# Attention and a mixture of experts: the third list's search moved, its rows turned by VectorE behind a DRAM scratch, one round's weight remainders subtracted on GpSimd

## Chip, cores and metric

One core of a Trainium2 chip runs the whole program. The metric is device time in microseconds (us) of one execution; the time given for a kernel is the median of its runs.

## What is computed

Attention over 8 batches, 8 heads, 576 positions and 64 columns with two masks (a window of 32, and a window of 128 at every fourth position), then a mixture of experts on its 4608 x 512 result. The routing is greedy over all (token, expert) pairs in falling order of the gate's logits, with 576 places for each expert:

```python
x = attn_out.transpose(0, 2, 1, 3).reshape(4608, 512)
logits = x @ w_gate                              # 4608 x 8
for idx in np.argsort(-logits.flatten()):
    tok, e = idx // 8, idx % 8
    if assigned[tok] >= 0 or counts[e] >= 576:
        continue
    assigned[tok] = e
    counts[e] += 1
for e in range(8):
    mask = assigned == e
    out[mask] = np.maximum(x[mask] @ w1[e], 0.0) @ w2[e]     # w1 512 x 1024, w2 1024 x 512
```

## The kernel before

The attention comes first (`attention`, to about 178 us of the span) and writes x to DRAM (`xd`) row by row. One expert's list is found by `alone` without anything beside it. After that the kernel runs eight rounds; round r computes one expert's 576 tokens, and the lists of later rounds are searched on VectorE beside the products of the rounds before.

**A round's products.** Everything is multiplied in pairs of a high part (rounded to the short float format of TensorE's fast path) and a low part (what the rounding left), so each product is three: high by high, high by low, low by high. The first product (`first`, L1460) makes 1024 hidden rows in eight pieces f, each for 256 (j = 0) and 320 (j = 1) tokens: per piece and j 12 instructions of 256 or 320 columns. The second (L1506, L1509, L1511) runs over five blocks m of 128, 128, 128, 128 and 64 tokens: 112 instructions of 512 columns. All of this is one chain on TensorE in the order of the rounds.

**What a round needs.** (1) Its list: `search(r)` makes eight steps. In each, TensorE counts (`counts`, L841, nine small matmuls) what VectorE flagged (`step`, L889 to L899, and the flags G, L853, L855 or L1176). Then `members`, `ranks` (TensorE), `accept`, `digits`; then `within` (six instructions that write `ob`, VectorE), `by_chunk` (`rx`, GpSimd, L1181) and `by_row` (ScalarE) feed `place` (TensorE, L1195), and `indices` (VectorE, L1204 to L1207) leaves the list as row numbers `idx`. (2) Its rows x: `gather` fetches them with one indirect DMA a block, issued by GpSimd. In rounds 0 to 2 (r < QUARTERS) TensorE turns a block with four transposes into PSUM (`ptx`, L1396), ScalarE writes the high part `xh` from there and VectorE the low part `xl` (L1245). From round 3 on `spread` is used: the gathered block goes to a DRAM scratch (`ROWS`, L1420) and comes back in four pieces (L1424), so arranged that one VectorE transpose of 32 x 32 squares (L1430) ends with the tokens along the free axis; the weights are then read from a copy of W1 with its rows permuted alike (`in_moe_w1q`). (3) Its weights: `weights` loads 128 x 512 blocks into `raw`, ScalarE writes the high part, and the low part is either subtracted by VectorE (L1245) or, for the pairs in ADDED, written as minus the high part by ScalarE (L1271) and then completed by a GpSimd DMA that adds `raw` onto it (L1273).

**What sets the order.** `Schedule` plans all engines ahead from a table of costs and due times: each operation has a cost, dependencies, and a boost that makes it due earlier, and the finished plan is the fixed order of each engine. T_P is the assumed cost of one count, B_C the boost of the search of list r, B_L that of the list's making, AHEAD the number of rounds that a search may run ahead. In `search`, `hold` is what a search must wait for; for r = 2 it is the first product of round 1.

```python
hold = gemm1_end.get(r - AHEAD) if r != 2 else gemm0[1]
g = prev + [hold]
```

**Queues.** SyncE (SP) issues the plain transfers in its planned order: the weights, the scratch stores and loads, and a register load of the expert's number (`fetch`) that waits for the end of a search. GpSimd issues the gathers, the adding DMAs and the scatters of the results (`put`, L1532), each behind a memset of `spacer`.

Of the kernel before, what the change touches and what calls it, by code (L numbers as in the profile page):

```python
# [32 lines left out]
NM = 5  # L33
# [4 lines left out]
HI16, LO16 = -4128832, 4128831  # L38
HIGH = 65536.0
TOL_DVE, TOL_ACT, TOL_POOL, TOL_PE, T_W = 100, -50, 200, 500, 730  # L40
T_P, T_S, AHEAD = 310, 2200, 5
B_L, B_G, B_T, B_X, B_H, B_HL, B_Y, B_S, B_W = 23000, 27000, 15000, 0, 20000, 17000, 28000, -15000, 1500
RAW1, D_R, NQ, AHEAD_W = 8, 262, (2, 2), (3, 4)
QUARTERS, POOLED, T_B, T_H, B_R = 3, range(0), 5000, 2500, 20000
ADDED, T_A, T_G, T_L = (("2", 0), ("1", 1), ("2", 1)), 4500, 4500, 3500
T_D = {"1": 5000, "2": 4000}
NS, B_E, DIRECT, T_I = (2, 2), 3000, 7, 5000
B_C = (0, 2500, *(20000 + -16000 * (r >= QUARTERS) for r in range(2, 8)))
P_U, B_A, B_K, B_V, B_P, TOL_A, TOL_B, TOL_C, TOL_D = 4680, 15400, -5200, 14500, -105500, 650, 650, 300, 800
Q_ENG = (("POOL", "POOL", "POOL", "ACT"), ("DVE", "DVE", "ACT", "ACT"))  # L50
MSZ = (128, 128, 128, 128, 64)
# [119 lines left out]
class Schedule:  # L171
# [9 lines left out]
    def op(self, eng, cost, fn, deps=(), boost=0, lat=0, dma=0, buf=None, mode=64, tail=None):  # L181
        x = Op(len(self.ops), eng, cost, fn, deps, boost, lat, dma, buf)
        x.mode = mode
        x.tail = self.LAT if tail is None else tail
        for d in x.deps:
            d.users.append(x)
        self.ops.append(x)
        return x
# [1023 lines left out]
def moe(tc, ctx, C, R, xd, ROWS, w1, w1q, w2, out):  # L1212
# [8 lines left out]
    op = K.op  # L1221
# [11 lines left out]
    XG = [pw.tile([128, DM // (1 + (i == 4))], F32, name=f"xg{i}") for i in range(NM + 2)]  # L1233
    XU = [[] for _ in XG]
# [11 lines left out]
    E, gemm1_end, x_users, got, gate = {}, {}, {}, {}, {}  # L1246

    def weights(n, r, f, deps):
# [15 lines left out]
        ld = op("SP", 60, load, [*deps, *old], dma=T_W, lat=T_D[n] if r > 1 else T_L if n == "1" and r in gate and r else 0)  # L1264
# [4 lines left out]
        if (n, r) in ADDED:  # L1269
            use.append(hi)  # L1270
            ne = op("ACT", 525, lambda: nc.scalar.activation(l, h.bitcast(F32), AF.Copy, scale=-1.0), [hi, *oldl], B_W)  # L1271
            useh.append(ne)
            lo = op("POOL", 1040, lambda: nc.gpsimd.dma_start(l, raw, accum_op=OP.add), [ne], B_W, lat=T_A)  # L1273
            use.append(lo)
        elif n == "2" and r >= 2 and f in POOLED:
            lo = op("POOL", 1350, lambda: sub(nc.gpsimd, l, raw, h), [ld, hi, *oldl], B_W)
            use += [hi, lo]
        else:
            lo = op("DVE", 600, lambda: sub(nc.vector, l, raw, h), [ld, hi, *oldl, st["list"] if first else None], B_W)
            use += [hi, lo]  # L1280
# [9 lines left out]
    def search(r):  # L1290
        scan.append(r)
        prev = st["next"]
        hold = gemm1_end.get(r - AHEAD) if r != 2 else gemm0[1]
        g = prev + [hold]
        for v in range(2):
            for it in range(4):
# [12 lines left out]
                g = [chain("DVE", cost, dve, [p, *g[1:]], early)]  # L1309
# [34 lines left out]
    def listing(r, sl):  # L1344
        d = st["digits"] = op("DVE", 485, R.digits, [sl, st["place"]], B_L)
        t, old, use = PTR.take()
        lows, c1 = [], 0
        for n in OB[r > 0]:
            c0, c1 = c1, c1 + n
            lows.append((op("DVE", 110 + (36 if r == 0 else 26) * n, lambda c0=c0, c1=c1: R.within(c0, c1), [d], B_L), c0, c1))  # L1350
        halves = [(0, 14), (14, NCH)] if r == 0 else [(0, NCH)]
        xs = [(op("POOL", 150 + (30 if r == 0 else 18) * (c1 - c0), lambda c0=c0, c1=c1: R.by_chunk(c0, c1), [d], B_L),
               op("ACT", 250 + 9 * (c1 - c0), lambda c0=c0, c1=c1: R.by_row(c0, c1), [d], B_L)) for c0, c1 in halves]
# [53 lines left out]

    def spread(r, m, n, a, b, wx, full, ix, box):

        rows, k = XG[NM + m % 2], n // 32  # L1410
        xg = XG[m][:, :128 * k]

        def get():
            nc.gpsimd.indirect_dma_start(out=rows[:n], out_offset=None, in_=xd,  # L1414
                                         in_offset=bass.IndirectOffsetOnAxis(ap=box[0][:n, m:m + 1], axis=0))

        g = op("POOL", 1250, get, [ix, *XU[NM + m % 2]], B_G, lat=T_B)

        back = ROWS[r % 2][m]
        sd = op("SP", 400, lambda: nc.sync.dma_start(back[:n], rows[:n]), [g, *RU.get((r - 2, m), [])], B_R, dma=T_W, lat=T_H)  # L1420
# [3 lines left out]
                nc.sync.dma_start(xg[32 * q:32 * q + 32].rearrange("t (x c) -> t x c", x=k),  # L1424
                                  back[:n, 128 * q:128 * q + 128].rearrange("(x t) c -> t x c", t=32))

        ld = op("SP", 1800, move, [sd, *XU[m]], B_R, dma=T_W, lat=T_H)
        RU[r, m] = [ld]
        XU[NM + m % 2] = [sd]
        t = op("DVE", 60 + 5 * n, lambda: nc.vector.transpose(xg, xg), [ld], B_T)  # L1430
        xt, a, b = (*(y.rearrange("p d (x i) -> p d x i", i=32) for y in (b, a)), xg.rearrange("p (x d i) -> p d x i", d=ND, i=32))[::-1]
        s0 = op("ACT", full, lambda: act(a, xt), [t, *wx], B_T)
# [214 lines left out]
```

## Time and profile before

| | |
|---|---|
| median of 3 runs | 651.45 us (650.06 to 654.1) |
| the profiled execution | 653.12 us |
| its span, first to last instruction | 651.4 us |
| TensorE busy in the span | 618.2 us (95%) |
| VectorE, ScalarE, GpSimd busy | 463.3, 304.4, 212.0 us |

The profile is of one execution; its span is 1.7 us shorter than its own time. The rounds' products begin at 205.7 us of the span and end at 646.3 us. Busy times are sums of a stretch; matmuls overlap, so a row's length on TensorE is longer than its share, and the distance from one start to the next is the cost.

### The profile page before, as it was taken

What the parts mean: (1) busy time and instruction counts of PE and PEld (TensorE: products, weight loads), DVE (VectorE), ACT (ScalarE), POOL (GpSimd) and SP (SyncE); (2) the same over time, 40 slices, a digit from 0 to 9 for tenths busy, and PEclk for the clock granted to TensorE, in tenths of its full rate; (3) what the DMA queues carried; (4) which work ended last, traced back from release to release, by engine and by line L of the source; (5) the groups of instructions that cost most, each with busy time, mean ns of one, the idle gap of its engine ahead of it and who ended that gap; (6) DMA issues with size and microseconds to landing.
All of it is one profiled execution on the core that took longest, in us unless ns stands there. A gap on an engine that the chain in (4) does not pass through costs nothing.

```text
span 651.4 us, 18440 instructions
## 1 busy us (share of the span) xinstructions
PE 618.2 (95%) x7084; PEld 538.6 (83%) x7084; DVE 463.3 (71%) x1566; ACT 304.4 (47%) x675; POOL 212.0 (33%) x316
## 2 busy tenths in 40 slices
PE   7899899999858999999999999999999999999996
PEld 5788788879645988997799789789879979988985
DVE  4667577777678884799899999889889765624300
ACT  5676566666303825754445155235325425524211
POOL 6356467566004317333221221213112142011011
PEclk9899899999957999999999999999999999999999
DMA  8888898887206837997258338417716977302001
GB/s 240 228 245 238 236 261 253 218 244 203 80 3 191 222 82 195 284 189 253 76 157 273 107 109 268 156 62 254 212 41 211 272 229 234 107 34 73 1 25 48
DMA packets 68008, 110.97 MB, mean 170 GB/s; under 512 B 9168, under 2 KB 30544, under 8 KB 67920
## 3 DMA queue, kind: packets, MB, share of 16 engines
q1 hardware_dynamic: 58576, 84.62, 43.4%
q0 software_dynamic: 9344, 25.17, 14.5%
q8 instruction: 55, 0.90, 0.6%
q14 instruction: 33, 0.27, 0.1%
HBM read 78.69 MB, written 24.77 MB: 159 GB/s over the span
## 4 chain that ended last, share of the span: by engine, by line
PE 79%; DVE 8%; issue 5%; ACT 3%; DMA 2%; POOL 2%; SPq 0%; POOLq 0%; DVEq 0%; ACTq 0%
PE ph L1460 28%; PE py L1506 23%; PE px L550 4%; PE pS L538 4%; PE px L609 3%; PE py L1509 2%; PE py L1511 2%; PE pz L841 2%; PE pm L526 1%; PE pS L533 1%; PE pm L522 1%; PE pz L927 1%; DMA const<-in_cf 1%; POOL xg L1382 1%; PE ptx L1195 1%
## 5 line engine op out<-in xcount | busy, mean ns | idle before, releaser
L1506 PE MATMUL py<-w2h,hb 128*128 128x512 f32 x512 | 168.5, 396 | 0.0
L1460 PE MATMUL ph<-xh,w1h 128*128 128x256 f32 (+1 forms) x512 | 137.6, 299 | 0.8 <-ACT xh L1244 0.7
L1460 PE MATMUL ph<-xh,w1l 128*128 128x256 f32 (+1 forms) x512 | 136.2, 297 | 0.0
L1460 PE MATMUL ph<-xl,w1h 128*128 128x256 f32 (+1 forms) x512 | 136.2, 296 | 0.0
L1506 PEld LDWEIGHTS py<-w2h,hb 128*128 128x128 f32 x512 | 96.2, 188 | 18.9
L1244 ACT ACTIVATE hb<-ph 128x320 fp32r<-128x320 f32 (+2 forms) x192 | 59.8, 346 | 92.2 <-PE ph L1460 88.8
L1506 PE MATMUL py<-w2l,hb 128*128 128x512 f32 x256 | 99.8, 390 | 0.0
L1460 PEld LDWEIGHTS ph<-xh,w1h 128*128 128x128 f32 x512 | 91.9, 190 | 1.8 <-ACT xh L1244 0.9
L1460 PEld LDWEIGHTS ph<-xh,w1l 128*128 128x128 f32 x512 | 91.7, 190 | 0.1
L1460 PEld LDWEIGHTS ph<-xl,w1h 128*128 128x128 f32 x512 | 91.6, 190 | 0.0
L1532 POOL DMA_INDIRECT out<-y,idx x40 | 40.8, 1020 | 152.9 <-ACT y L1244 119.2
L1481 DVE SCALAR_TENSOR_TENSOR hb<-ph,hb 128x320 fp32r<-128x320 f32 (+1 forms) x128 | 57.0, 454 | 32.3 <-ACT hb L1244 29.5
L1244 ACT ACTIVATE y<-py 128x512 f32<-128x512 f32 (+1 forms) x40 | 23.9, 598 | 102.6 <-PE py L1506 91.3
L1414 POOL DMA_INDIRECT xg<-xd,idx x25 | 29.1, 1162 | 98.3 <-DMA rows<-xg 81.1
L492 ACT ACTIVATE E<-pS 128x384 f32<-128x384 f32 x96 | 44.9, 492 | 28.0 <-PE pS L538 27.3
L1506 PEld LDWEIGHTS py<-w2l,hb 128*128 128x128 f32 x256 | 48.2, 188 | 8.4
L550 PE MATMUL px<-v,E 128*64 128x65 f32 x1152 | 48.7, 224 | 5.0 <-issue 3.8
L538 PE MATMUL pS<-q,k 128*64 128x64 f32 x1152 | 53.0, 229 | 0.0
L550 PEld LDWEIGHTS px<-v,E 128*64 128x64 f32 x1152 | 42.4, 137 | 9.7 <-issue 5.8
L318 POOL COPY v<-v 32x520 f32<-32x520 f32 (+2 forms) x56 | 34.1, 633 | 49.1 <-DMA v<-in_vp 20.5
L538 PEld LDWEIGHTS pS<-q,k 128*64 128x64 f32 x1152 | 48.7, 144 | 0.0
L1245 DVE TENSOR_TENSOR w2l<-raw,w2h 128x512 fp32r<-128x512 f32 x48 | 31.7, 684 | 23.2 <-ACT w2h L1244 22.9
(217 smaller groups left out, 1123.6 us busy)
## 6 DMA issues: line engine op xcount, KB each, us to landing
raw<-in_moe_w SPq DMA_DIRECT2D x88, 256.0 KB
raw<-in_moe_w1q SPq DMA_DIRECT2D x40, 256.0 KB
rows<-xg SPq DMA_DIRECT2D x20, 256.0 KB
xg<-rows SPq DMA_DIRECT2D x80, 64.0 KB
qs<-in_qp SPq DMA_DIRECT2D x16, 288.0 KB
k<-in_kp SPq DMA_DIRECT2D x16, 288.0 KB
qs<-in_qd SPq DMA_DIRECT2D x16, 288.0 KB
k<-in_kd SPq DMA_DIRECT2D x16, 288.0 KB
```

Of the source, the lines that this page charges most:

```text
L318: f(t[:32, c0 + 1:c1 + 1], t[96:, c0:c1])
L492: e = self.op("ACT", 475, lambda j=j, pS=pS: nc.scalar.activation(self.E[:, 3 * j:3 * j + 3].rearrange("p c x -> p (c x)"), pS.tile[:, :38 ...
L538: x = nc.tensor.matmul(pS[64 * h:64 * h + 64, k, :, h], self.K[:, 32 * g:32 * g + 64], self.Q[:, g], start=False, stop=True, skip_group_ch ...
L550: x = nc.tensor.matmul(px[64 * h:64 * h + 64, c - c0, a], self.E[:, k, 64 * a:64 * a + 64], self.V[:, k, 2 * self.ui + a], start=True, sto ...
L609: x = nc.tensor.transpose(pt.tile[:, 128 * (c - c0):128 * (c - c0) + 128], xs[:, c, 2 * ui:2 * ui + 2].rearrange("p a d -> p (a d)"), C["i ...
L1244: act = lambda o, i, f=AF.Copy: nc.scalar.activation(o, i, f)
L1245: sub = lambda e, o, a, b: e.tensor_tensor(o, a, b, op=OP.subtract)
L1414: nc.gpsimd.indirect_dma_start(out=rows[:n], out_offset=None, in_=xd, in_offset=bass.IndirectOffsetOnAxis(ap=box[0][:n, m:m + 1], axis=0))
L1460: nc.tensor.matmul(o, a[:, d * 128:d * 128 + 128], b[:, d, c0:c1], start=((d, i) == pairs[0]), stop=((d, i) == pairs[-1]))
L1481: hl = op("DVE", 335 if j == 0 else 400, lambda: nc.vector.scalar_tensor_tensor(hb[:, CAP + c0:CAP + c1], o, 0.0, hb[:, c0:c1], op0=OP.max ...
L1506: nc.tensor.matmul(py, x, w, start=(f + i == 0), stop=(f == NF - 1 and i == 2))
L1532: s = nc.gpsimd.indirect_dma_start(out=out, out_offset=bass.IndirectOffsetOnAxis(ap=box[0][:n, m:m + 1], axis=0), in_=y[:n], in_offset=None)
```

## The change

Round 2 goes over to `spread` (QUARTERS from 3 to 2) and reads the permuted W1. Its first four blocks are gathered right into the tile that later takes the turned block (`XG[m]`), not into the two shared row tiles, so all five gathers can be under way together. The search of list 2 no longer waits for the first product of round 1. The low parts of W2 in round 1 are subtracted by GpSimd; the eight negated copies on ScalarE and the eight adding DMAs of that round go. The planner's numbers change too: T_P from 310 to 280, the boosts of the searches, and a smaller boost B_O for the six `within` of list 2. From line 1409 on the lines of the changed kernel are one higher.

```diff
-QUARTERS, POOLED, T_B, T_H, B_R = 3, range(0), 5000, 2500, 20000
-ADDED, T_A, T_G, T_L = (("2", 0), ("1", 1), ("2", 1)), 4500, 4500, 3500
+QUARTERS, T_B, T_H, B_R = 2, 5000, 2500, 20000
+ADDED, T_A, T_G, T_L = (("2", 0), ("1", 1)), 4500, 4500, 3500
...
-        elif n == "2" and r >= 2 and f in POOLED:
+        elif (n, r) == ("2", 1):
             lo = op("POOL", 1350, lambda: sub(nc.gpsimd, l, raw, h), [ld, hi, *oldl], B_W)
             use += [hi, lo]
...
-        hold = gemm1_end.get(r - AHEAD) if r != 2 else gemm0[1]
+        hold = gemm1_end.get(r - AHEAD)
...
-        rows, k = XG[NM + m % 2], n // 32
+        at, k = m if r == 2 and m < 4 else NM + m % 2, n // 32
+        rows = XG[at]
...
-        g = op("POOL", 1250, get, [ix, *XU[NM + m % 2]], B_G, lat=T_B)
+        g = op("POOL", 1250, get, [ix, *XU[at]], B_G, lat=T_B)
...
-        ld = op("SP", 1800, move, [sd, *XU[m]], B_R, dma=T_W, lat=T_H)
+        ld = op("SP", 1800, move, [sd, *(XU[m] if at != m else ())], B_R, dma=T_W, lat=T_H)
         RU[r, m] = [ld]
-        XU[NM + m % 2] = [sd]
+        XU[at] = [sd]
```

The order on three places. VectorE at the end of round 0 in the kernel before: G is the flags of the first step of list 2, the xl are the low parts of round 1's rows, the rows from L889 on are a step of the search.

```order
L960 TENSOR_TENSOR oh<-Lt,Mo 128x288
L853 TENSOR_TENSOR G<-V,const_65 128x36x16
L1245 TENSOR_TENSOR xl<-ptx_3700,xh 128x4x128 x4
L889 STREAM_TRANSPOSE Q<-pz 128x128
L891 TENSOR_REDUCE q<-Q 128x8
L894 TENSOR_SCALAR junk,flag<-q 128x8
```

The same place now, from the second step's flags to the second xl.

```order
L1176 TENSOR_TENSOR G<-e,const_64 128x36x16
L870 TENSOR_SCALAR R<-R,delta 128x36
L1245 TENSOR_TENSOR xl<-ptx_3700,xh 128x4x128
L889 STREAM_TRANSPOSE Q<-pz 128x128
L891 TENSOR_REDUCE q<-Q 128x8
L894 TENSOR_SCALAR junk,flag<-q 128x8
L896 STREAM_TRANSPOSE F<-flag 128x32
L899 TENSOR_SCALAR F_4994,delta<-F 128x32
L877 TENSOR_SCALAR e<-R,delta 128x72
L1176 TENSOR_TENSOR G<-e,const_64 128x36x16
L870 TENSOR_SCALAR R<-R,delta 128x36
L1245 TENSOR_TENSOR xl<-ptx_3700,xh 128x4x128
```

Four xl in a row stood ahead of the search; now the second to the sixth step of the search have one xl behind each.

GpSimd in round 1 before: the last adding DMAs of W2 (w2l from raw), the list's rx, a scatter, and the five gathers of round 2's rows (xg).

```order
L1273 DMA w2l_3745<-raw_3711 128x512
L1273 DMA w2l_3746<-raw_3712 128x512
L1181 TENSOR_TENSOR rx<-oa,const_64 128x36x10
L1531 MEMSET spacer 1x1
L1532 DMA out<-y_3766,idx 4608x512
L1382 DMA xg_3747<-xd,idx 128x512
L1382 DMA xg_3748<-xd,idx 128x512
L1382 DMA xg_3749<-xd,idx 128x512
L1382 DMA xg_3750<-xd,idx 128x512
L1382 DMA xg_3752<-xd,idx 64x512
```

The same place now.

```order
L1245 TENSOR_TENSOR w2l_3745<-raw_3711,w2h_3729 128x512
L1245 TENSOR_TENSOR w2l_3746<-raw_3712,w2h_3730 128x512
L1181 TENSOR_TENSOR rx<-oa,const_64 128x36x10
L1532 MEMSET spacer 1x1
L1533 DMA out<-y_3765,idx 4608x512
L1415 DMA xg_3747<-xd,idx 128x512
L1415 DMA xg_3748<-xd,idx 128x512
L1415 DMA xg_3749<-xd,idx 128x512
L1415 DMA xg_3750<-xd,idx 128x512
L1415 DMA xg_3752<-xd,idx 64x512
```

The two DMAs have become two subtractions (the last of eight), and the scatter ahead of the gathers is that of round 0's last block (y_3765), no longer that of round 1's first (y_3766).

VectorE where round 2 begins, before: the last step of the search of list 3, with the low part of round 2's last block (xl, 64 tokens) in it.

```order
L1245 TENSOR_TENSOR xl<-ptx_3700,xh 128x4x128
L889 STREAM_TRANSPOSE Q<-pz 128x128
L891 TENSOR_REDUCE q<-Q 128x8
L894 TENSOR_SCALAR junk,flag<-q 128x8
L896 STREAM_TRANSPOSE F<-flag 128x32
L899 TENSOR_SCALAR F_5944,delta<-F 128x32
L1245 TENSOR_TENSOR xl<-ptx_3700,xh 128x4x64
L1031 TENSOR_SCALAR s<-const_65,delta 128x2
```

The same place now: oa and ob are digits of list 3, L1431 turns the blocks of round 2, and idx is list 3.

```order
L1176 TENSOR_TENSOR oa<-si,const_64 128x360
L1431 STREAM_TRANSPOSE xg_3747<-xg_3747 128x512
L1431 STREAM_TRANSPOSE xg_3748<-xg_3748 128x512
L1176 TENSOR_TENSOR ob<-si,const_64 128x384 x6
L1245 TENSOR_TENSOR xl<-xg_3747,xh 128x4x128
L1245 TENSOR_TENSOR xl<-xg_3748,xh 128x4x128
L1204 COPY t_6043<-ptx_3700 64x20
L1205 TENSOR_TENSOR t_6043<-t_6043,ptx_3700 64x20
L1207 SCALAR_TENSOR_TENSOR idx<-t_6043 64x5 x2
L1431 STREAM_TRANSPOSE xg_3749<-xg_3749 128x512
L1431 STREAM_TRANSPOSE xg_3750<-xg_3750 128x512
L1431 STREAM_TRANSPOSE xg_3751<-xg_3751 128x256
```

The search of list 3 is over by then, and the turning of round 2's five blocks stands around the making of list 3: two blocks ahead of ob, three behind idx.

## Rows read from the trace of the kernel before

**Rows 1.** The page: the chain that ended last, shares of the span by engine.

```profile
PE 79%; DVE 8%; issue 5%; ACT 3%; DMA 2%; POOL 2%; SPq 0%; POOLq 0%; DVEq 0%; ACTq 0%
```

**Rows 2.** Busy us by window: PE, PEld, DVE, ACT, POOL; PEclk, DMA share, GB/s.

```profile
264.10:293.50 29.40, 29.27 (x271) 28.44 (x270) 25.91 (x118) 19.92 (x47) 11.48 (x14) 1.00 0.96 225
293.50:324.80 31.30, 30.89 (x221) 24.00 (x220) 28.27 (x116) 14.14 (x27) 10.78 (x14) 1.00 0.50 167
```

**Rows 3.** Timeline of TensorE around one turned block: start, us, engine, line.

```profile
262.29 0.60 PE L1396 MATMUL ptx<-const,xg 128*128 128x128 f32 x4
262.65 0.48 PE L1509 MATMUL py<-w2h,hb 128*128 128x512 f32 x1
262.97 0.40 PE L1511 MATMUL py<-w2l,hb 128*64 128x512 f32 x1
263.20 0.39 PE L1509 MATMUL py<-w2h,hb 128*128 128x512 f32 x1
```

**Rows 4.** Timeline of TensorE in round 1: two waits beside the search of list 3.

```profile
311.39 0.40 PE L1506 MATMUL py<-w2h,hb 128*128 128x512 f32 x1
311.98 0.42 PE L841 MATMUL pz<-G,ohr 128*128 128x64 bf16 x9 [0.19 <-issue]
...
318.38 0.44 PE L841 MATMUL pz<-G,ohr 128*128 128x64 bf16 x9
319.03 0.66 PE L1396 MATMUL ptx<-const,xg 128*128 128x128 f32 x4 [0.22 <-DVE xl L1245]
```

**Rows 5.** Timelines of TensorE and ScalarE in round 0: list 1 placed, copies for the counts.

```profile
246.93 0.48 PE L1506 MATMUL py<-w2h,hb 128*128 128x512 f32 x1
...
250.30 1.16 ACT L982 ACTIVATE ohr<-oh 128x1152 bf16<-128x1152 bf16 x1 [0.74 <-DVE oh L960]
```

**Rows 6.** Timelines of TensorE and VectorE: one count and the step behind it.

```profile
308.80 0.44 PE L841 MATMUL pz<-G,ohr 128*128 128x64 bf16 x9
...
309.60 0.32 DVE L889 STREAM_TRANSPOSE Q<-pz 128x128 f32<-128x128 f32 x1 [0.17 <-PE pz L841]
...
311.17 0.76 DVE L853 TENSOR_TENSOR G<-V,const 128x576 bf16<-128x576 f32 x1
311.84 0.68 DVE L1245 TENSOR_TENSOR xl<-ptx,xh 128x512 fp32r<-128x512 f32 x1
```

**Rows 7.** List 3 placed (from the chain), and the first two gathers of round 3.

```profile
332.19 0.56 PE ptx L1195 x18
...
334.74 0.99 POOL L1414 DMA_INDIRECT xg<-xd,idx  x1 [3.58 <-DVE hb L1481]
336.04 1.43 POOL L1414 DMA_INDIRECT xg<-xd,idx  x1 [0.30 <-issue]
```

**Rows 8.** Timeline of SP's queue: scratch stores and loads of round 3.

```profile
340.18 0.36 SPq L1420 DMA_DIRECT2D rows<-xg  x1
...
345.03 3.67 SPq L1424 DMA_DIRECT2D xg<-rows  x8
...
352.85 0.81 SPq L1420 DMA_DIRECT2D rows<-xg  x2
359.01 3.72 SPq L1424 DMA_DIRECT2D xg<-rows  x8
```

**Rows 9.** Groups by line with shapes: count, busy us, mean ns, idle before.

```profile
L1430 DVE STREAM_TRANSPOSE xg<-xg 128x512 f32<-128x512 f32 x20 | 13.7, 698 | 2.0 <-DMA xg<-rows 1.9
...
L1244 ACT ACTIVATE xh<-xg 128x512 fp32r<-128x512 f32 x20 | 12.3, 631 | 12.3 <-DMA rows<-xg 4.1 <-DVE idx L1207 3.2 <-DVE xg L1430 2.0
```

**Rows 10.** Groups of GpSimd; then timelines of GpSimd and VectorE as list 3 is made.

```profile
L1273 POOL DMA_DIRECT2D w2l<-raw x16 | 14.0, 872 | 23.9 <-ACT w2l L1271 15.3 <-ACT hb L1244 8.7
...
L1181 POOL TENSOR_TENSOR rx<-oa,const 128x360 bf16<-128x360 bf16 x7 | 5.7, 817 | 34.3 <-DVE oa L1176 34.3
...
330.32 0.84 POOL L1181 TENSOR_TENSOR rx<-oa,const 128x360 bf16<-128x360 bf16 x1 [7.31 <-DVE oa L1176]
...
330.15 1.49 DVE L1176 TENSOR_TENSOR ob<-si,const 128x384 bf16<-128x384 int16 x3
```

More of the change, by code (lines that the diff above doesn't have):

```diff
@@ L40 @@
 TOL_DVE, TOL_ACT, TOL_POOL, TOL_PE, T_W = 100, -50, 200, 500, 730
-T_P, T_S, AHEAD = 310, 2200, 5
-B_L, B_G, B_T, B_X, B_H, B_HL, B_Y, B_S, B_W = 23000, 27000, 15000, 0, 20000, 17000, 28000, -15000, 1500
+T_P, T_S, AHEAD = 280, 2200, 5
+B_O, B_L, B_G, B_T, B_X, B_H, B_HL, B_Y, B_S, B_W = 10000, 23000, 27000, 15000, 0, 20000, 17000, 28000, -15000, 1500
 RAW1, D_R, NQ, AHEAD_W = 8, 262, (2, 2), (3, 4)
-QUARTERS, POOLED, T_B, T_H, B_R = 3, range(0), 5000, 2500, 20000
-ADDED, T_A, T_G, T_L = (("2", 0), ("1", 1), ("2", 1)), 4500, 4500, 3500
+QUARTERS, T_B, T_H, B_R = 2, 5000, 2500, 20000
+ADDED, T_A, T_G, T_L = (("2", 0), ("1", 1)), 4500, 4500, 3500
 T_D = {"1": 5000, "2": 4000}
 NS, B_E, DIRECT, T_I = (2, 2), 3000, 7, 5000
-B_C = (0, 2500, *(20000 + -16000 * (r >= QUARTERS) for r in range(2, 8)))
+B_C = (0, 3500, 20000, 20000, 12000, 12000, 12000, 4000)
 P_U, B_A, B_K, B_V, B_P, TOL_A, TOL_B, TOL_C, TOL_D = 4680, 15400, -5200, 14500, -105500, 650, 650, 300, 800
@@ L1349, in listing @@
             c0, c1 = c1, c1 + n
-            lows.append((op("DVE", 110 + (36 if r == 0 else 26) * n, lambda c0=c0, c1=c1: R.within(c0, c1), [d], B_L), c0, c1))
+            lows.append((op("DVE", 110 + (36 if r == 0 else 26) * n, lambda c0=c0, c1=c1: R.within(c0, c1), [d], B_O if r == 2 else B_L), c0, c1))
         halves = [(0, 14), (14, NCH)] if r == 0 else [(0, NCH)]
```

## The prediction

> **What bounds the kernel now.** I read the page's chain first: TensorE carries 79% of it [rows 1]. Then the busy times by window: in the first product of round 1 TensorE is busy 29.27 of 29.40 us, in its second 30.89 of 31.30, at full clock [rows 2]. Then TensorE's own timeline, to see whether those sums hide waits: products of 512 columns start 0.23 us apart without a hole [rows 3], and beside the search of list 3 there are two short holes. A product that starts at 311.39 should be followed at 311.62, and the count comes at 311.98: 0.36 us. The nine matmuls of the count at 318.38 take some 0.27 us (the next start behind the count at 311.98 is of that size), so the turning at 319.03 waits 0.38 us, for a low part [rows 4]. So between 205.7 and 646.3 us TensorE's instruction stream is the time. An edit gains what it takes out of that stream and the waits that it closes, and loses what it makes TensorE wait; nothing else counts.
>
> **The change part by part.** *Turning by VectorE.* The 20 transposes of round 2 leave TensorE. One block costs 0.36 us (262.29 to 262.65), and the product behind it takes 0.32 us, not 0.23, before the next starts [rows 3]: 0.45 us. Five blocks: 2.25 us; the last has 64 tokens, so 2.0 at the least. Gain 2.25.
>
> *The two waits of rows 4.* Both belong to the stretch that is put together anew: the turning that waited is gone, and the count now stands elsewhere. Gain 0.73, bounds 0 and 0.74.
>
> *The search of list 2 moved into round 0.* Five of its eight counts now stand among round 0's second products. A count costs the same there; what can be late is what it waits for. The first stands 18 products behind the placing of list 1. Products go on at 246.93, so TensorE is there at about 251.1. The copies that it multiplies are ready at 250.30 + 1.16 = 251.46 [rows 5]. ScalarE starts them as soon as VectorE has written oh, so they can't come sooner: a wait of 0.35. Then one cycle: from a count's start to the step's start 0.80, to the end of the flags 2.33 (309.60 to 311.93), together 3.13 before the next count can begin [rows 6]; steps without the added low half are some 0.3 shorter. In the new order TensorE has about 2.9 to 3.3 us of products, counts and turnings between two of these counts, so they come out even, from 0 to 0.3 late each. One place is worse: there is one PSUM tile for turning, and the second block of round 1 waits until VectorE has written the first block's xl, which now stands behind a step. Counted from the second count: 0.80 + 2.0 + 0.2 + 0.68 for the xl [rows 6], that is 3.7. TensorE arrives after nine products, one turning and two counts of 0.36 (0.27 and 0.09 of reloading), that is 3.2 to 3.3. Wait 0.3 to 0.4; I take 0.3.
>
> *The search of list 3 in round 1.* VectorE is the tight engine here: 28.27 of 31.30 us before [rows 2]. Going through its rows in the new order in the same way I find one late count, behind the sixth step, where TensorE has only 2.4 us for a cycle that needs 2.8: 0.4.
>
> *Round 2's rows through DRAM.* Let P be the start of placing list 2. In round 3 placing begins at 332.19 and the first gather at 334.74; gathers go out 1.30 apart [rows 7]. Here all five go at once: the last starts at P + 2.6 + 5.2 = P + 7.8. A gather is in SBUF when its store is issued, 334.74 to 340.18, 5.4 us [rows 7, 8]: the fifth store at P + 13.2. SP issues stores first and then 20 loads at 3.67/8 = 0.46 us: loads of blocks 0 and 1 are out by P + 17.3, all by P + 22.8. From a store to the load behind it took 4.85 us (340.18 to 345.03) and 6.2 (352.85 to 359.01) [rows 8]; no row shows a load's landing alone, so I bound it by 2.5, half of the shorter of these, and 6.2, and take 4.85. Blocks 0 and 1 are back by P + 22.2 (19.8 to 23.5), all by P + 27.7 (25.3 to 29). VectorE's turn is 0.70 a block, ScalarE's high part 0.63 [rows 9]. In the new order 106 products, five counts, one ranking and two placings stand between P and round 2: some 27 us. Its first product needs blocks 0 and 1 at P + 27, and blocks 2 to 4 after 24 products of 0.12, at P + 30. Data is there in time by 1 to 3 us. What is short is VectorE: the turns of blocks 2 to 4 stand behind idx of list 3, which stands behind a placing that ends 0.5 us before round 2. 0.2 for the semaphore, 0.75 for idx, 0.70 + 0.70 + 0.44 for three turns and 0.4 for the last high part make 3.2 after that end, against 3.4. With the xl ahead of idx it is 3.7. Wait 0.3; bounds 0 and 1.5 (the slow landing).
>
> A price from a page beside that row: the Trainium skill, "DMA: Bandwidth & Descriptors", section "Anatomy of one DMA — SWDGE (gpsimd) path", gives a fixed 2.0 us and the bytes at 436 GB/s, an estimate of 2.6 us for such a gather. The row has 5.4, and the measurement decides; by the page the rows would be back 2.8 us sooner, and the sum would stand where it is, less at most this 0.3.
>
> *W2's low parts by GpSimd.* Eight adding DMAs of 0.87 us go from GpSimd, and eight subtractions of 128 x 512 come, which no row shows. Nearest is rx at 0.82 us for 360 elements [rows 10]: not below 0.8, by its rate 1.2, and double that, 2.3, for elements of twice the bytes. I take 1.2, so 9.6 in all (6.4 to 18.4). GpSimd was busy 11.48 of 29.40 us with the DMAs in it [rows 2], so 14 to 23 of 29: hidden, before list 2 is placed and before W2 is used. VectorE pays too: as rx ran for 0.84 us, three ob took 1.49, where the group's 0.35 each would be 0.9 [rows 10]. Subtracting on GpSimd holds up VectorE's instructions with two SBUF inputs by about as long as it runs. In that window VectorE had 25.91 of 29.40 [rows 2]; five steps of 2.3 leave it, up to 9.6 of holding comes: 24. Hidden. Cost 0.
>
> This is also the rule that speaks against the change: the Trainium skill, "SBUF — State Buffer", section "Who interferes with whom", says that a VectorE instruction with two SBUF inputs contends with GpSimd's reads, and that the loser blocks fully. The trace agrees: 0.6 of 0.84 us.
>
> *The sum.* 2.25 + 0.73 - 0.35 - 0.3 - 0.4 - 0.3 = 1.6 us gained. The profiled execution, 653.12 us, of which the span is 651.4, would take 651.5. It stands 1.7 over the median of the runs shown, 651.45, so the median goes to 649.9.
>
> **Rivals.** *Nothing is gained (651.4).* The plan now assumes shorter counts, so counts may come too early all along. For: rows 4 have such a wait of 0.36 already, and eight of them beside the search of list 2 make 2.9, which with the 0.3 at round 2's start gives back 2.25 + 0.73. Against: the six searches of before show only two waits of that size. *Slower (654.5).* GpSimd's subtraction at 2.3 us. Then VectorE is held for 18.4 and has 25.9 - 11.7 + 18.4 = 32.6 for 29.4: 3.2 late in round 1, hidden parts late for TensorE, and list 2 late by as much, of which 1.5 comes out again at round 2's start: -1.6 + 4.7 = +3.1. It decides from 1.9 us a subtraction (29.4 - 14.2 = 15.2, over eight). For: two inputs of full width, unseen here. Against: rx's rate, and ScalarE, not VectorE, starts the hidden parts. *More gained (648.5).* All new waits close: 2.25 + 0.73 = 3.0. For: they are small differences of sums; against: the copies' 0.35 rests on one row. *It doesn't take effect:* out, since the order shows the transposes gone from a TensorE that has no idle time under them.
>
> **How the numbers follow.** Forecast 0.55, nothing gained 0.25, slower 0.12, more gained 0.08. Runs of one kernel spread from 650.06 to 654.1, so a median of three can lie 1.5 off. From 648.5 less 1.5 to the last but one case, 651.4, with the spread and half of the slower case: 647.0 to 653.8. A measurement of this kernel tells about 1% from no change, 6.5 us; none of the gains reaches that, and the slower case would only if both its bounds and the DRAM path's fell together: faster 0.02, same 0.93, slower 0.05.
>
> **What would show it.** Right: no L1396 for round 2 on TensorE; the first count of list 2 close behind the ohr copy, with a wait of some 0.3; W2's low parts in round 1 as GpSimd TENSOR_TENSOR near 1.2 us; round 2's first product about 1.6 us sooner than before. Wrong: a wait of over 2 us of TensorE at round 2's start on DMA xg or on ScalarE's xh, subtractions of 2 us or more, or waits at the counts adding up to over 3 us.

## The result and the profile after

| | before | after |
|---|---|---|
| median | 653.07 us (6 runs, 650.06 to 656.33) | 660.12 us (6 runs, 658.11 to 663.87) |
| ratio to the kernel before | | 1.0116, interval 1.0072 to 1.016 |
| span of the profiled execution | 651.4 us | 656.3 us |
| mean granted clock of TensorE | 0.975 | 0.971 |

The change made the kernel 7 us slower, just over 1%. The forecast was 649.9 us, 1.6 us faster than the 651.45 of the three runs known then, with a range up to 653.8.

First the chain that ended last, to be read against [rows 1]:

```profile
PE 69%; issue 11%; DVE 10%; DMA 6%; ACT 2%; POOL 1%; SPq 1%; POOLq 0%; DVEq 0%; ACTq 0%
```

TensorE carries 10 points less of it than before, so it has begun to wait. Where, the busy times by window tell. The columns are those of [rows 2]; the first two rows are round 1's first and second product, the others pieces of 2 us of the first:

```profile
263.90:298.90 35.00, 30.90 (x245) 30.08 (x245) 30.78 (x108) 19.72 (x46) 14.57 (x14) 0.90 0.62 187
298.90:330.00 31.10, 29.35 (x206) 22.72 (x206) 26.52 (x111) 6.74 (x13) 10.31 (x14) 1.00 0.61 191
...
276.00:278.00 2.00, 2.00 (x18) 1.96 (x16) 1.90 (x6) 1.63 (x5) 2.00 (x3) 1.00 0.00 0
278.00:280.00 2.00, 0.23 (x2) 0.10 (x1) 2.00 (x2) 0.28 (x1) 2.00 (x2) 1.00 0.11 10
280.00:282.00 2.00, 0.05 (x2) 0.04 (x2) 1.93 (x7) 0.00 (x0) 0.17 (x1) 0.63 0.80 281
282.00:284.00 2.00, 2.00 (x10) 2.00 (x10) 1.90 (x10) 0.00 (x0) 0.00 (x0) 0.50 0.96 276
286.00:288.00 2.00, 2.00 (x12) 2.00 (x12) 1.00 (x6) 0.38 (x1) 0.03 (x1) 0.66 1.04 381
```

The first product, 29.40 us long before with all of search 2 in it, takes 35.0 us now with less to do. From 278.2 to 282 TensorE does nothing, VectorE is busy throughout and GpSimd until 280.2, and then the granted clock is at 0.50, the lower of the two levels, until about 287. TensorE's timeline at that place:

```profile
277.92 0.31 PE L1461 MATMUL ph<-xl,w1h 128*128 128x320 f32 x1
281.95 0.22 PE L1118 MATMUL pz<-ge,const 128*128 128x72 bf16 x1 [3.73 <-DVE ge L1075]
282.04 0.61 PE L1461 MATMUL ph<-xh,w1h 128*128 128x320 f32 x1
282.45 0.47 PE L1461 MATMUL ph<-xh,w1l 128*128 128x320 f32 x1
```

The ranks of list 2 (L1118) wait for `ge`, the last of VectorE's short instructions between the search's last step and the ranks. Here are five of those instructions, and GpSimd beside them:

```profile
273.99 1.23 DVE L1032 TENSOR_TENSOR PR<-s,q 128x16 f32<-128x16 f32 x1
275.97 0.51 DVE L1046 SCALAR_TENSOR_TENSOR fe<-Z,const 128x8 f32<-128x8 f32 x1
276.70 1.03 DVE L1058 TENSOR_SCALAR ohe<-fe,em 128x8 bf16<-128x8 f32 x1
277.89 1.10 DVE L1024 TENSOR_SCALAR gg<-R,delta 128x36 bf16<-128x36 f32 x1
278.90 1.30 DVE L1025 TENSOR_SCALAR gg<-R,delta 128x36 bf16<-128x36 f32 x1
...
269.30 1.29 POOL L1245 TENSOR_TENSOR w2l<-raw,w2h 128x512 fp32r<-128x512 f32 x1
271.22 8.95 POOL L1245 TENSOR_TENSOR w2l<-raw,w2h 128x512 fp32r<-128x512 f32 x7 [0.63 <-ACT w2h L1244]
```

PR works on 16 elements a partition and takes 1.23 us. GpSimd's eight subtractions are nearly one block from 269.3 to 280.2, some 1.29 us each, and the chain runs right beside it. The second place is in the second product, at the fifth of the gathers of round 2's rows:

```profile
307.34 1.33 POOL L1415 DMA_INDIRECT xg<-xd,idx  x1 [0.30 <-issue]
307.58 0.43 PE L841 MATMUL pz<-G,ohr 128*128 128x64 bf16 x9
308.97 1.03 POOL L1533 DMA_INDIRECT out<-y,idx  x1 [0.22 <-issue]
310.07 0.32 DVE L889 STREAM_TRANSPOSE Q<-pz 128x128 f32<-128x128 f32 x1 [2.18 <-issue]
312.22 0.42 PE L841 MATMUL pz<-G,ohr 128*128 128x64 bf16 x9 [1.40 <-DVE G L855]
```

A count starts at 307.58 and lasts 0.43 us, but VectorE begins the step behind it only at 310.07, after 2.18 us in which the profile shows nothing that it waits for. The next count is late by that, 1.56 us behind the pace of the products. I call this VectorE's stand.

The account, from round 0's first product to the last of round 7: 440.1 us before (205.73 to 645.84), 447.6 now (203.26 to 650.82), 7.5 more. (The span grew by only 4.9, since the rounds begin 2.5 us sooner in this execution.) The ranks wait 3.9. The 22 products between 282.04 and 287.39 take 5.35 us, where ten of 0.147 and twelve of 0.12 at full clock make 2.9: 2.4. A count just ahead (270.99), whose flags G took 1.61 us beside the first subtraction: 0.5. The stand: 1.6. Four smaller waits, told below, 1.8 together. These are 10.2; less the 2.25 of the transposes and the 0.73 of the two old waits they make 7.2, and 0.3 net I can't place.

### The profile page after: what moved, and what is told of

Read it like the earlier page. It is cut to its first block, busy times and chain, and to the rows that moved or that the text cites. A ratio compares the mean times of both kernels' runs of the same rounds, so it can differ in the third digit from the quotient of the medians.

```text
span 656.3 us, 18439 instructions
## 1 busy us (share of the span) xinstructions
PE 616.3 (94%) x7064; PEld 537.2 (82%) x7064; DVE 470.1 (72%) x1571; ACT 300.3 (46%) x667; POOL 213.9 (33%) x316
## 4 chain that ended last, share of the span: by engine, by line
PE 69%; issue 11%; DVE 10%; DMA 6%; ACT 2%; POOL 1%; SPq 1%; POOLq 0%; DVEq 0%; ACTq 0%
PE ph L1461 22%; PE py L1507 21%; PE px L550 4%; PE pS L538 4%; PE px L609 2%; PE pz L841 2%; DMA rows<-xg 2%; PE py L1512 2%; PE py L1510 2%; DMA xg<-rows 2%; PE pS L533 1%; PE pm L526 1%; DMA qs<-in_qd 1%; PE pm L522 1%; PE pz L927 1%
## 5 line engine op out<-in xcount | busy, mean ns | idle before, releaser
L1482 DVE SCALAR_TENSOR_TENSOR hb<-ph,hb 128x320 fp32r<-128x320 f32 (+1 forms) x128 | 57.3, 453 | 34.1 <-ACT hb L1244 31.8
L1415 POOL DMA_INDIRECT xg<-xd,idx x30 | 33.3, 1109 | 111.4 <-DMA rows<-xg 83.0
L492 ACT ACTIVATE E<-pS 128x384 f32<-128x384 f32 x96 | 44.7, 492 | 28.3 <-PE pS L538 27.6
```

What stands on the lines that cost most here:

```text
L492: e = self.op("ACT", 475, lambda j=j, pS=pS: nc.scalar.activation(self.E[:, 3 * j:3 * j + 3].rearrange("p c x -> p (c x)"), pS.tile[:, :38 ...
L1482: hl = op("DVE", 335 if j == 0 else 400, lambda: nc.vector.scalar_tensor_tensor(hb[:, CAP + c0:CAP + c1], o, 0.0, hb[:, c0:c1], op0=OP.max ...
```

## The experiments

Two theories stand against each other for the larger part. One: GpSimd's subtractions hold VectorE on the way to the ranks. The other: the earlier search, planned with shorter counts, is late by itself. Ratios are to the kernel before on the same chip; its median there lay between 652 and 657 us, so ratios are compared, not times.

**The changed kernel again (after_again).** No edit.

> The changed kernel once more, beside the next two on one chip. If its loss is a matter of the program and not of the first chip, the ratio to the kernel before lies again between 1.007 and 1.016, the ranks of list 2 wait 3.5 to 4 us and the granted clock of round 1's first product is 0.90.

Measured: 1.0076 (1.0047 to 1.0105). The ranks wait 3.89 us to the next start, as before; the stand is 3.2 us this time, and its count 2.64 us late. The granted clock of the first product is 0.95, not 0.90, so what the clock costs differs from one execution to the next; the wait doesn't. The loss is the program's.

**The subtractions left out (e1_no_subs).**

```diff
-            lo = op("POOL", 1350, lambda: sub(nc.gpsimd, l, raw, h), [ld, hi, *oldl], B_W)
+            lo = op("POOL", 1350, lambda: nc.gpsimd.memset(l[:1, :1].bitcast(F32), 0.0), [ld, hi, *oldl], B_W)
```

> The eight subtractions of W2's low parts on GpSimd in round 1 are replaced by eight memsets of one element, so the low parts of round 1's W2 are left out; every other instruction and its order stay as in the changed kernel. Theory (GpSimd's subtractions hold VectorE's instructions on the way to list 2's ranks, and the idle TensorE then loses its clock): the wait of 3.7 us before the ranks is gone, the granted clock in round 1's first product is 1.00 and not 0.90, that product takes about 28.5 us and not 34.9, and the time falls by 6 to 7 us, to 653 to 654 us. Rival (the new place of the search, or counts planned too short, makes the wait): ranks still wait 2 us or more and the time stays within 1.5 us of 660.

Measured: 0.9993 (0.9962 to 1.0024). The same instructions of VectorE in this run's timeline:

```profile
278.72 0.18 DVE L1032 TENSOR_TENSOR PR<-s,q 128x16 f32<-128x16 f32 x1
279.64 0.17 DVE L1046 SCALAR_TENSOR_TENSOR fe<-Z,const 128x8 f32<-128x8 f32 x1
280.04 0.23 DVE L1058 TENSOR_SCALAR ohe<-fe,em 128x8 bf16<-128x8 f32 x1
280.42 0.22 DVE L1024 TENSOR_SCALAR gg<-R,delta 128x36 bf16<-128x36 f32 x1
280.56 0.23 DVE L1025 TENSOR_SCALAR gg<-R,delta 128x36 bf16<-128x36 f32 x1
...
282.79 0.21 PE L1118 MATMUL pz<-ge,const 128*128 128x72 bf16 x1
```

The five took 5.17 us beside the subtractions and take 1.03 here: 4.1 us, about the wait of the ranks. The ranks don't wait at all now (`ge` ends at 282.71, they start at 282.79), the clock is at 1.00 throughout the first product, and that product is 28.2 us long instead of 35. The plan is the same, so the first theory holds and the second falls. The ratio fell by 0.8 to 1.2 points, 5 to 8 us.

**TensorE kept at work while it waits (e3_fill).**

```diff
-            rk = chain("PE", 70, R.ranks, [m], B_L)
+            rk = chain("PE", 70, (lambda: (keep_clock(nc, R.zero, PTR.tiles[0], 16), R.ranks())) if r == 2 else R.ranks, [m], B_L)
```

> Sixteen products of zeros (512 columns of the short format, some 0.22 us each, 3.5 in all) are put on TensorE right ahead of list 2's ranks, so that TensorE works while it waits there; all else stays as in the changed kernel. Theory: VectorE reaches the ranks no sooner, so the ranks come at the same distance from round 1's start (within 0.3 us), but the granted clock behind them stays at 1.00 and the 23 products that ran at half pace (5.35 us for 3.05) run at full: 2.3 us less, 657 to 658 us. Rival 1 (the clock fell for another reason than the idle engine): it falls again, no gain. Rival 2 (the wait was not for VectorE): the ranks come later by what the fill takes, 3 us, and the time rises.

Measured: 1.0041 (1.0012 to 1.007). Round 1's first product by window:

```profile
268.04:300.66 32.62, 31.92 (x259) 29.22 (x259) 30.32 (x105) 19.74 (x46) 14.53 (x14) 1.00 0.66 202
```

The ranks come 18.0 us after the round's start (286.05 less 268.04), as in the changed kernel (281.95 less 263.95), so the wait is still there; but the clock stays at 1.00 and the product is 32.6 us long, 2.3 less than the 34.9 from 263.95 to 298.88. That separates the two prices: 3.9 us for the wait, 2.3 to 2.4 for the clock that the idle engine lost.

**VectorE subtracts itself (e5_vector).**

```diff
-        elif (n, r) == ("2", 1):
+        elif False:
```

> The same eight low parts by VectorE (0.68 us each, 5.5 us in all), the plan made anew. Theory: five short instructions of the search wait 4.1 us for GpSimd in the changed kernel, while the planner can put VectorE's own subtractions between them, so the ranks come 1 to 4 us sooner than in the changed kernel and TensorE keeps its clock: 654 to 657 us. Rival (any 5 us more in that stretch make list 2 as late): 659 us or more.

Measured: 1.0101 (1.0042 to 1.0159). The time is the rival's, its reason is not: the ranks come 13.6 us after the round's start (269.18 to 282.78), 4.4 sooner than in the changed kernel, and don't wait. What is late are counts of list 3. In the plan made anew three of them, at 298.49, 301.24 and 304.52, follow each other with no product between them; they wait 1.0, 1.7 and 2.6 us for their flags, and the first product takes 35.8 us:

```profile
301.24 0.64 PE L841 MATMUL pz<-G,ohr 128*128 128x64 bf16 x9 [1.69 <-DVE G L1176]
304.52 0.64 PE L841 MATMUL pz<-G,ohr 128*128 128x64 bf16 x9 [2.64 <-DVE G L853]
...
304.38 0.69 DVE L1245 TENSOR_TENSOR w2l<-raw,w2h 128x512 fp32r<-128x512 f32 x1
```

The first of VectorE's eight subtractions starts at 304.38, behind the flags of all three counts. So the run shows that the new plan is a bad one; it doesn't show what VectorE's own subtractions would cost in place of the holding.

**The subtractions alone, in the kernel before (e9_before_subs).**

```diff
-ADDED, T_A, T_G, T_L = (("2", 0), ("1", 1), ("2", 1)), 4500, 4500, 3500
+ADDED, T_A, T_G, T_L = (("2", 0), ("1", 1)), 4500, 4500, 3500
...
-        elif n == "2" and r >= 2 and f in POOLED:
+        elif (n, r) == ("2", 1):
```

> The kernel before with GpSimd's eight subtractions in place of the adding DMAs of W2 in round 1, nothing else (the plan made anew with the same numbers). Theory: all eight counts of list 2 stand in round 1's first product there, their steps are held as well, so counts or ranks are late by 3 to 8 us and the time is 3 to 10 us above the kernel before (1.005 to 1.015). Rival (the subtractions hurt only together with the earlier search, which puts the list's making beside them): within 2 us of the kernel before.

Measured: 1.0037 (1.0003 to 1.0071), 2.4 us, between the ranges of the theory and of the rival, and its interval takes in parts of both. The trace decides, with a first product of round 1 of 39.6 us for 29.4. GpSimd, VectorE and TensorE there:

```profile
271.05 7.52 POOL L1245 TENSOR_TENSOR w2l<-raw,w2h 128x512 fp32r<-128x512 f32 x6
272.15 6.48 DVE L877 TENSOR_SCALAR e<-R,delta 128x72 int16<-128x72 f32 x1
278.66 0.46 DVE L1176 TENSOR_TENSOR G<-e,const 128x576 bf16<-128x576 int16 x1
279.17 0.64 PE L841 MATMUL pz<-G,ohr 128*128 128x64 bf16 x9 [6.52 <-DVE G L1176]
```

One instruction of 0.26 us (e, L877) took 6.48: it was held to the end of the row of subtractions, not of the one at work. In the changed kernel each of the five came through at the end of the one at work, though there too seven subtractions of some 1.29 us follow each other within 8.95; what makes the difference is not shown. The place of the search changes which instruction is hit, not that one is. The profiled execution loses more than the ratio says; the profile is one execution, the ratio twelve.

**GpSimd copies instead of subtracting (e4_copy).**

```diff
-            lo = op("POOL", 1350, lambda: sub(nc.gpsimd, l, raw, h), [ld, hi, *oldl], B_W)
+            lo = op("POOL", 1350, lambda: nc.gpsimd.tensor_copy(l, raw), [ld, hi, *oldl], B_W)
```

> GpSimd's eight subtractions become eight copies of raw (one SBUF input instead of two; W2's low parts of round 1 are thereby replaced by W2 itself), in the same order as in the changed kernel. Theory in its first form (two reading sides that want the same port): a copy holds VectorE as long as it runs, so the five short instructions of the search (0.17 to 0.23 us alone) again take 0.5 to 1.3 us each and the ranks wait in proportion to the copies' time. Rival (only instructions with two SBUF inputs on GpSimd's side hold VectorE): these five take 0.17 to 0.23 us, the ranks wait less than 0.3 us and the granted clock in round 1's first product is 1.00.

Measured: 659.94 us (one run; the kernel before 655.97). Neither case came as written. The copies need no high part, run earlier, and hit the step before the chain:

```profile
270.74 3.68 POOL L1276 CAST w2l<-raw 128x512 fp32r<-128x512 f32 x6
270.86 3.62 DVE L877 TENSOR_SCALAR e<-R,delta 128x72 int16<-128x72 f32 x1
```

Six copies in a row held one instruction of VectorE for their whole length, and a count waited 2.6 us. So one SBUF input on GpSimd's side is enough.

**The adding DMAs again (e2_adding_dma).**

```diff
-ADDED, T_A, T_G, T_L = (("2", 0), ("1", 1)), 4500, 4500, 3500
+ADDED, T_A, T_G, T_L = (("2", 0), ("1", 1), ("2", 1)), 4500, 4500, 3500
```

> W2's low parts of round 1 by eight negated copies on ScalarE and eight adding DMAs again, as before the change; everything else of the change stays, and the plan is made anew. Theory: no GpSimd instruction holds VectorE, so ranks of list 2 wait less than 0.6 us and the time is 651 to 654 us: the rest of the change is worth between 0 and 2 us of gain, its 2.25 us of transposes against late counts. Rival (the rest of the change is what costs): 658 us or more.

Measured: 1.0028 (0.9991 to 1.0064). The ranks don't wait, but a new stop came, on ScalarE:

```profile
294.15 0.63 ACT L1244 ACTIVATE w2h<-raw 128x512 fp32r<-128x512 f32 x1 [4.15 <-DMA raw<-in_moe_w]
...
296.44 1.22 DVE L1482 SCALAR_TENSOR_TENSOR hb<-ph,hb 128x320 fp32r<-128x320 f32 x3 [3.27 <-ACT hb L1244]
```

List 2's expert is known earlier, so SP issues W1 of round 2 ahead of the last blocks of W2 of round 1. ScalarE waits for W2, the hidden parts behind it wait, VectorE waits for those, and a count is 3.2 us late, with a half clock behind it.

**W2 of round 1 first (e11_w2_first, e11_again).** The run before plus one dependency:

```diff
+        if (n, r) == ("1", 2):
+            deps = [*deps, lds[7]]
```

`lds` holds the loads of round 1's W2.

> As the run with the adding DMAs, and W1 of round 2 is loaded behind W2 of round 1 (a dependency on W2's last load). In that run ScalarE waited for W2's blocks at 294 us behind seven blocks of W1, VectorE and a count behind it, 3.2 us with some 1.6 us of half clock after it. Theory: this wait is gone, and the time falls by 3 to 5 us to 0.995 to 0.999 of the kernel before. Rival (W1 of round 2 then comes too late): a wait of 2 us or more at round 2's start, and no gain.

> The version with the adding DMAs and W1 of round 2 behind W2 of round 1 once more, to see whether its ratio of 0.994 to the kernel before comes again. Theory of the sum (2.25 us of transposes and 0.7 us of waits against late counts of some 1.5 us): 0.995 to 1.000. Rival (the first measurement holds more than that, since the kernel before has waits too that its profile does not show): 0.991 to 0.995.

Measured: 0.994 (0.9912 to 0.9968) and on another chip 0.9995 (0.9963 to 1.0028). The windows of round 1's two products in the first:

```profile
265.30:293.41 28.11, 28.11 (x245) 27.47 (x244) 25.16 (x105) 22.22 (x50) 11.26 (x14) 1.00 0.99 244
293.41:322.68 29.27, 29.18 (x206) 22.65 (x205) 26.78 (x112) 8.95 (x18) 11.23 (x14) 1.00 0.75 231
```

Both parts of the loss are gone, and round 1 takes 57.4 us instead of 61.4 before the change; but round 0, with five more counts in it, takes 61.2 for 58.4, and round 2 56.2 for 55.0. From the first product to the last it is 440.1 us, as in the kernel before. One interval lies below 1, the other around it: a small gain of this version is possible, and not shown.

**The scratch alone, in the kernel before (e8_before_spread).** QUARTERS from 3 to 2, nothing else.

> The kernel before with one number changed: round 2 already by the DRAM scratch and VectorE's turning (QUARTERS 2), with the two shared row tiles, the adding DMAs and the old search. Theory of the sum (20 transposes off TensorE are worth 2.25 us): between 0.5 and 2.5 us faster than the kernel before if the rows are back in time. Rival (with list 2 placed only some 21 us of products ahead of round 2 and gathers two at a time, the rows come late): TensorE waits 5 us or more at round 2's start and the time is above that of the kernel before by 2 us or more.

Measured: 1.0247 (1.0214 to 1.0279). This is no measure of the scratch: in the kernel before the table B_C is computed with QUARTERS, and the boost of search 2 fell from 20000 to 4000 with it. The search came late: TensorE waited 3.0 us for a placing in round 1's first product, and in round 2's 3.7 us for ranks and 3.0 for a placing. The worth of the 20 transposes was not measured by itself.

Now the stand. First theory: the end of a stretch of VectorE's code, since it came at the 937th recorded instruction in four runs.

**VectorE's code shifted (e10_shift16, e10_shift64).** On the run without subtractions:

```diff
-        nc.vector.memset(ONE, 1.0)
+        for _ in range(17): nc.vector.memset(ONE, 1.0)
```

and 65 in the second.

> As the run without subtractions (W2's low parts of round 1 left out there too), with sixteen more VectorE memsets at the program's very start; the order is the same otherwise. In the runs so far VectorE stood 1.0 to 3.2 us ahead of the same instruction (the transposition Q at the 937th recorded VectorE instruction, 306.6 us) though what it waits for was long done, and TensorE's count waited 1.6 to 2.7 us for it. Theory (VectorE comes to the end of a stretch of its code there and the next stretch is late while five gathers fill the DMA engines): the stand moves to an instruction 16 earlier in the program, some 4 us sooner, and is of another length. Rival (what runs beside that instruction, a scatter and a gather on GpSimd, holds it): it stays at the same Q, with 2 to 3.3 us.

> The same with sixty-four more memsets. Theory of the code's end: the stand at that Q is gone; the end of the stretch falls some 17 us sooner, at about 290 us, where the DMA engines have less to do, so the stand is below 0.5 us there, TensorE loses neither the 2.7 us of waiting nor the 2 us at half clock behind it, and the time is 2 to 5 us below the run without subtractions (0.993 to 0.997 of the kernel before). Rival (GpSimd's scatter and gather): the stand stays at the same Q and the time is that of the run without subtractions, within 1.5 us.

Measured: 664.45 us (one run) and 1.0273 (1.0248 to 1.0298). The stand stayed at the same Q, now the 953rd and the 1001st instruction, with 3.19 and 3.20 us. The theory fell. (The time of the second is no answer to anything else: its memsets delay the program's start, and round 0 begins at 218.8 us.)

**Gathers in two tiles (e6_two_tiles).**

```diff
-        rows = XG[at]
+        rows = XG[NM + m % 2]
```

> As the run without subtractions (W2's low parts of round 1 left out there too), but round 2's rows are gathered into two tiles in turn, so that the third to fifth gather wait for the scratch store two ahead; the order of every engine stays. Theory (five gathers at once delay what VectorE gets from TensorE): the stand of 3.2 us ahead of Q is below 1 us, TensorE's count after it does not wait, but the rows are back 5 us or more later and round 2's first product waits 2 us or more for them. Rival (the stand has nothing to do with the gathers' number): it stays at 2 to 3.3 us.

Measured: 654.9 us (one run; before 656.15), a second product of 29.24 us for 33.33 in the run without subtractions, at full clock. The third gather waits for the first to end, the fifth for the third, so two are under way and not five (none waits for a store, so the first blocks stored here hold rows of later ones):

```profile
304.62 0.95 POOL L1415 DMA_INDIRECT xg<-xd,idx  x1 [1.88 <-DMA xg<-xd,idx]
...
308.10 0.43 PE L841 MATMUL pz<-G,ohr 128*128 128x64 bf16 x9
308.11 1.21 POOL L1415 DMA_INDIRECT xg<-xd,idx  x1 [1.09 <-DMA xg<-xd,idx]
308.57 0.32 DVE L889 STREAM_TRANSPOSE Q<-pz 128x128 f32<-128x128 f32 x1
```

The count stands to the fifth gather as it does in the run without subtractions, and VectorE takes its result after 0.47 us: no stand, and no row too late in round 2. (Round 2's first product is 1.1 us longer than in the run without subtractions, 28.3 for 27.2, because of a late count at 350.37 and not of its rows.)

**The train of gathers moved (e13_delay5, e13_delay15, e16_gap5, e16_gap15).** On the run without subtractions:

```diff
         def get():
+            [nc.gpsimd.memset(spacer, 0.0) for _ in range(15 * ((r, m) == (2, 1)))]
```

with 5 or 15 memsets, ahead of the first gather (m = 0, e13) or of the second (m = 1, e16).

> As the run without subtractions (W2's low parts of round 1 left out), with five memsets of one element on GpSimd ahead of round 2's first gather, some 0.5 us, so that all five gathers start 0.5 us later against VectorE and TensorE. In six runs VectorE's stand ended 3.55 to 3.58 us after the start of the fifth gather, and the count it stood behind was then 0.22 to 0.26 us behind that start. Theory (the stand belongs to the train of gathers): it ends again 3.5 to 3.6 us after the fifth gather's start, so it is longer by 0.5 us or falls on another count. Rival (it belongs to that VectorE instruction or to TensorE's count): 3.2 us again, ending 3.0 to 3.1 us after the fifth gather's start.

> The same with fifteen memsets, some 1.5 us. Theory (train of gathers): the stand is another one, over 1 us different from 3.2 us, or on the next count, or gone, and still ends 3.5 to 3.6 us after the fifth gather's start. Rival (the instruction): 3.2 us at the same instruction.

> As the last two, but the five memsets stand between the first and the second gather, where GpSimd can't run them ahead of time (in the last two it did so while it waited for the list, and the gathers were not delayed at all). The second to fifth gather start 0.5 us later against VectorE. Theory (train of gathers): the stand ends again 3.5 to 3.6 us after the fifth gather's start, 0.5 us longer, or it falls on another count or away. Rival (the instruction): 3.1 to 3.2 us again, ending about 3.0 us after that start.

> The same with fifteen memsets, 1.5 us. Theory: the stand differs by over 1 us from 3.2 us, or falls on the next count, or is gone. Rival: 3.1 to 3.2 us again.

One run each: 662.32 and 656.58 us, where the kernel before took 652.47, and 655.02 and 657.82, where it took 654.57. The first two did not move the gathers: GpSimd ran the memsets while it waited for the list. The stand was 3.09 and 3.07 us at the same Q. The other two did. In the last one:

```profile
305.81 0.44 PE L841 MATMUL pz<-G,ohr 128*128 128x64 bf16 x9
306.29 0.32 DVE L889 STREAM_TRANSPOSE Q<-pz 128x128 f32<-128x128 f32 x1
...
307.94 1.23 POOL L1416 DMA_INDIRECT xg<-xd,idx  x1 [0.30 <-issue]
308.90 0.43 PE L841 MATMUL pz<-G,ohr 128*128 128x64 bf16 x9
311.34 0.32 DVE L889 STREAM_TRANSPOSE Q<-pz 128x128 f32<-128x128 f32 x1 [1.99 <-PE py L1508]
```

The count that had been late (305.81) is answered after 0.48 us; the next one, 0.96 us behind the fifth gather's start, after 2.4 us. With five memsets too it is the next count, 1.64 us behind that start, and the stand is 0.67 us. So it does not belong to that instruction: it moves with the train of round 2's gathers. It ended 3.4 us behind the fifth gather's start in the last run, 2.8 in the one with five memsets, 3.55 to 3.58 in six runs, 3.4 to 3.5 in the two of e13, 2.7 in the first profile of the changed kernel and 1.8 in e2, so the 3.5 to 3.6 of the expectation is no constant. And a train of five gathers is not enough to make a stand: in e11_w2_first and e11_again the count that starts 1.5 us behind the fifth gather was answered at once, and in round 0, whose rows come by five gathers 1.2 to 1.8 us apart, so was the count 1.0 to 1.8 us behind the fifth, within 0.05 us of its end, in all nineteen profiles. What hands TensorE's finished count so late to VectorE is not shown.

## Why the prediction was wrong

*What bounds the kernel* was right, and so was the rule drawn from it: what TensorE waits is the loss, and all but 0.3 us of it was found as TensorE's waits and its clock.

*The step that failed* is the last one of the sum, W2's low parts by GpSimd, "Hidden. Cost 0." Its size was right: 1.29 us a subtraction against the 1.2 taken, and the holding stayed below its bound of 9.6 us: 4.1 on five instructions and 1.1 on the flags G (1.61 us for 0.50 in the run without subtractions). The error was to set the holding against the idle time of a stretch of 29.4 us. The subtractions do not spread over it. They fall in one block of 11 us, one behind the other but for holes of 0.6 and 0.1 us, and that block lies on the chain from the search's last step to the ranks, where every instruction waits for the one before and TensorE waits for the last. Its slack was that of one chain: none (without the subtractions `ge` ends 0.08 us before the ranks start). The rival "slower" had the mechanism, but by the same sum it let it decide only from 1.9 us a subtraction; it decided at 1.29, with 3.9 us of wait. The clock was priced nowhere: an idle TensorE came back at the lower level, for 2.4 us more.

The Trainium skill, "SBUF — State Buffer", section "Who interferes with whom", which the prediction had cited for two inputs, says in the same section that `tensor_scalar` too can take the shared ports, in a mode that uses two of them. The trace agrees: three of the five instructions held are TENSOR_SCALAR, at 1.03 to 1.30 us for 0.23, and transposes, reductions and the hidden parts (L1482, 0.41 to 0.49) were not held. I had counted only instructions with two inputs.

*A second step failed by being absent.* The prediction let all five gathers go at once and followed their data, P + 7.8 for the last; they went within P + 6.8, and the rows were back in time. That a count beside the train could be late (1.6 us here, 2.6 and a half clock in the second profile) was in no term. The train itself is not new: the kernel before starts round 2's five gathers from 303.84 to 309.12 us, 1.3 us apart as here. But there one count starts 0.3 us ahead of the fifth gather and the next 2.9 us behind it; in the changed kernel one starts 0.24 us behind it.

*The terms on the other side* were sized well, if a little low. The first count waits 0.35 us for the ohr copy (forecast 0.35), the second block's turning 0.42 (0.3), the late count behind the sixth step 0.51 (0.4), round 2's second piece 0.54 for ScalarE's xh behind VectorE's turns (0.3):

```profile
248.20 0.39 PE L1507 MATMUL py<-w2h,hb 128*128 128x512 f32 x1
248.78 0.44 PE L841 MATMUL pz<-G,ohr 128*128 128x64 bf16 x9 [0.20 <-issue]
...
255.44 0.66 PE L1396 MATMUL ptx<-const,xg 128*128 128x128 f32 x4 [0.27 <-DVE xl L1245]
...
314.38 0.39 PE L1507 MATMUL py<-w2h,hb 128*128 128x512 f32 x1
315.12 0.42 PE L841 MATMUL pz<-G,ohr 128*128 128x64 bf16 x9 [0.35 <-issue]
...
333.39 0.86 PE L1461 MATMUL ph<-xh,w1h 128*128 128x320 f32 x4 [0.38 <-ACT xh L1244]
```

From 248.20 to 248.78 are 0.58 us where a product takes 0.23, and so on. The two old waits of [rows 4] are gone as said. With both losses taken out (e11) the gain of 1.6 us did not show in the profile either, 440.1 us for 440.1: a count at 402.97 us is late there by another 1.05, one at 307.85 by 0.25, and the earlier search makes rounds 0 and 2 longer.

*Of the other rivals*, "nothing gained" by counts that come too early all along did not come: no unforeseen count among search 2's in round 0 waited. The expectations that missed are told above; the one that cost most was e8, where one number moved two things.

## What to carry to other kernels

Time in which one engine holds another is not spread over a stretch: ask which chain runs beside the burst, and set the burst against that chain's slack, above all where the chain is made of short instructions that each pay the rest of a long one. Where TensorE is the bound, add to a wait of a few us what the clock costs behind it; here 3.9 us of idling cost 2.4 more. And when work moves (here the counts of a search), look at what else is under way beside its new place, not only at when its data is there.

## What the runs showed of the hardware that was not expected

- A row of GpSimd instructions held one short VectorE instruction to the end of the whole row: 6.48 us for an instruction of 0.26 beside six subtractions (e9), 3.62 beside six copies (e4). In the changed kernel the instructions held came through at the end of the subtraction at work; why it differs is not shown.
- In twelve profiles the result of a count that started between 0.02 us ahead of the fifth gather of round 2 and 1.64 us behind it reached VectorE 0.7 to 3.2 us late, and in e9, built on the kernel before, by 0.7 at 0.06 us ahead. In the two of e11 (1.5 us behind) it did not, nor with two gathers under way, nor beside round 0's five gathers.
- TensorE came back at the lower clock after idling 3.9 us, and after waits of 2.1 to 2.8 us in eight other profiles (0.52 from 312 to 314 us in the run without subtractions), but not after 2.6 us in e10_shift16 (1.00 from 313 to 322 us), nor after 1.6 us in the first profile of the changed kernel.
